# Expert 0's first layer in three column passes, with everything beyond 512 rows behind branches

## The chip, the cores and the metric

The kernel runs on one core of a Trainium2 chip. The metric is the device time of one execution in microseconds (us). The kernel before takes 761.73 us (median of 3 runs, 760.68 to 761.96).

A core has a matrix engine (TensorE, PE in the rows), a vector engine (VectorE, DVE), an engine for activation functions (ScalarE, ACT), GpSimd (POOL), which here also issues gathers and scatters, and SyncE (SP), which issues loads. Each engine works through its own instructions in order; they meet by semaphores.

## The reference

Attention with a causal mask and a bias from cumulated positive scores over 8 batches, 8 heads, 576 positions and head size 64; then a mixture of 8 experts over the 4608 rows of its output:

```python
cum = np.cumsum(np.maximum(s, 0.0), axis=-1)
scores = np.where(causal, -1e9, q @ k.T / sqrt(64) + np.minimum(-(cum[..., :, None] - cum[..., None, :]), 0.0))
x = softmax(scores) @ v                        # then 4608 rows x 512, all heads beside each other
logits = normalize(x) @ normalize(expert_emb).T / tau
expert = argmax(logits, 1); gate = softmax(logits)[expert]
for e in range(8):
    h = np.maximum(x[expert == e] @ w1[e], 0.0)   # 512 -> 1024
    out[expert == e] = gate * (h @ w2[e])         # 1024 -> 512
```

Results are float32.

## The kernel before, in words

The 64 pairs of batch and head are done one after the other in `step(n)`. When a batch is through, its rows are routed: `rank1` to `rank3` give every row a rank within its expert, and five scatters (L662, issued by GpSimd) write the rows to a list xs in HBM, each expert's part in order of rank.

An expert has at most 640 rows in five tiles t of 128. For each, `xload` gathers the rows (L730), `xtr` transposes them on TensorE (four f32 transposes, L756), `xcv` splits them in two float16 halves: xH by a cast on ScalarE (L762) and xL by a subtraction on VectorE (L764). `xstat` takes the sums that the gate needs: a square on ScalarE (L742) and three small operations on VectorE (L739, L740, L77); the gate's logits are nine more (L89 to L97), its weights four (L103 to L106).

Every product is of split float16 halves in three matmuls (xH with wH, xL with wH, xH with wL). The first layer is `l1(m, e, lo, hi)`, m = 0 to 7, 12 matmuls (L859) each over the columns lo to hi, followed by a Relu on ScalarE (L863) for the high half and a subtraction on VectorE (L864) for the low half of h. Its PSUM tile h comes from a pool of two. The second layer is `l2(e, t)`: 24 matmuls of 512 columns (L916), scaling on VectorE (L923) and a scatter to the output (L924).

Rows beyond 512 are a class of their own. `l1a` does the first layer of rows 512 to 575 in 96 matmuls of 64 columns (L882, in `lpart`), always. `l1b` does rows 576 to 639 behind a branch on TensorE and otherwise issues one matmul as a dummy (L900). `lrect` makes the Relu (L888) and the subtraction (L889) of either. `l2t` does tile 4 of the second layer: if there are over 576 rows with 24 full matmuls, if not with a dummy (L939) and 96 matmuls of 64 columns (L945), whose result `l2u` turns back by four transposes (L953) in the next expert. `classes` compares each expert's count with 576, `size` loads the result to TensorE.

Weights come by SyncE's queue (`wissue`), in tiles of 128x512 float32. ScalarE squares them (`wsq`, L814), a small chain gives a scale (`wnorm`, a matmul L825 and five or six operations L826 to L832), `wcv` converts to the high half on ScalarE (L842) and `wlow` takes the low half on VectorE (L850) and issues the load that reuses the space. With `hold`, `wcv` leaves its low halves in a list for a later `wlow`; without, it flushes the whole list.

Expert 0 starts before all rows are routed. When six batches are ranked, its next free rank is raised to at least SPL = 384, so that its first 384 rows don't change any more, and they are gathered as tiles 0 to 2. `l1(0..2)` over these columns stand in the tails of the last attention steps (64 to 66), `l1(3..7)` behind them, `l2(0, 0)` and `l2(0, 1)` follow, and in a second pass the columns 384 to 511, with `l1a(0)` behind m = 1 and `l2(0, 2)` behind m = 3. The order in every engine's queue is the order in which the code is written.

From the reference's inputs, expert 0 has 337 rows in the first six batches, 404 in seven, 468 in eight.

## Time and profile before

| | us |
|---|---|
| median of 3 runs (lowest, highest) | 761.73 (760.68, 761.96) |
| the profiled execution | 760.44 |
| its span, from the first to the last instruction | 758.3 |
| TensorE busy in it | 743.6 (98%) |
| VectorE, ScalarE, GpSimd busy | 527.9 (70%), 568.6 (75%), 393.8 (52%) |

The profile is of one execution. An engine's busy time is the union of its instructions; a row of the timeline gives the start, the length, the engine, the line and the tiles of an instruction or of several alike that follow one another, and in brackets how long the engine was idle before and whose end released it. Matmuls overlap: one that takes 0.38 us lets the next begin after 0.22, so prices are taken from start to start. Attention ends near 345 us; the change lies between about 320 and 403 us.

### The profile page before, as it was taken

The numbers are of one execution on the slowest core, as the hardware profiler recorded it, in microseconds if no ns is written. First come the engines' busy times: TensorE is split into PE (matmuls) and PEld (weight loads), VectorE is DVE, ScalarE is ACT, GpSimd is POOL, SyncE is SP. The second block draws the span as 40 slices with busy tenths as digits, with TensorE's granted clock in tenths as the row PEclk, the third lists the DMA queues.
The fourth block names the chain that finished last, engine by engine and source line by source line (L and its number), as shares of the span: only waits on it lengthen the run. The fifth ranks groups of instructions, "written<-read, shape, count | busy, mean of one in ns | idle before, by whom it ended". The sixth has DMA issues, their size and how long they took to land. (4 is left out here: it accounts for less than half of the span.)

```text
span 758.3 us, 21143 instructions
## 1 busy us (share of the span) xinstructions
PE 743.6 (98%) x8097; PEld 536.9 (71%) x8097; DVE 527.9 (70%) x1799; ACT 568.6 (75%) x1027; POOL 393.8 (52%) x375
## 2 busy tenths in 40 slices
...
GB/s 148 180 190 189 174 180 207 172 212 169 213 184 207 164 225 163 183 233 168 204 117 128 192 161 195 183 141 140 181 176 129 188 171 198 162 126 103 12 15 57
DMA packets 75993, 124.00 MB, mean 164 GB/s; under 512 B 38818, under 2 KB 39222, under 8 KB 75024
## 3 DMA queue, kind: packets, MB, share of 16 engines
...
## 5 line engine op out<-in xcount | busy, mean ns | idle before, releaser
L245 POOL TENSOR_TENSOR PL<-P 128x576 f16<-128x576 f32 (+2 forms) x128 | 204.5, 1718 | 12.5 <-ACT P L491 8.1
L859 PE MATMUL h<-xH,wt 128*128 128x512 f16 (+2 forms) x576 | 159.3, 355 | 0.7 <-DVE hq L864 0.2
L924 POOL DMA_INDIRECT out<-Kx,xj x39 | 43.7, 1122 | 201.3 <-DVE Kx L923 168.8
L859 PEld LDWEIGHTS <-wt 128*128 128x128 f16 x864 | 79.4, 98 | 83.8 <-issue 2.3
L519 PE MATMUL om<-vh,P 128*128 128x73 f16 x960 | 106.8, 199 | 0.9 <-DVE xt L544 0.6
L520 PE MATMUL om<-vl,P 128*128 128x72 f16 x960 | 106.2, 196 | 0.0
L521 PE MATMUL om<-vh,PL 128*128 128x73 f16 x960 | 106.0, 197 | 0.0
L355 PE MATMUL s<-qkb 96*128 96x288 f32 (+4 forms) x272 | 96.3, 368 | 1.5 <-DVE M L363 0.9
L730 POOL DMA_INDIRECT Qx<-xs,idx x40 | 44.3, 1106 | 99.4 <-ACT vjunk L814 56.1
L520 PEld LDWEIGHTS <-P 128*128 128x128 bf16 x960 | 94.7, 99 | 1.6 <-issue 1.1
L519 PEld LDWEIGHTS <-P 128*128 128x128 bf16 x960 | 93.7, 99 | 0.7 <-DVE xt L544 0.4
L521 PEld LDWEIGHTS <-PL 128*128 128x128 f16 x960 | 93.8, 98 | 0.0
L859 PE MATMUL h<-xL,wt 128*128 128x512 f16 (+1 forms) x256 | 90.5, 359 | 0.0
L916 PE MATMUL pxs<-wt,hq 128*128 128x512 f16 x360 | 88.8, 379 | 0.3 <-DVE wt L850 0.3
L916 PE MATMUL pxs<-wt,hp 128*128 128x512 f16 x288 | 77.8, 379 | 0.0
L363 DVE CUSTOM_DVE_ANT_0 junk<-s,mS 128x448 bf16<-128x448 f32 (+3 forms) x144 | 74.0, 521 | 5.1 <-PE s L355 2.8
L923 DVE TENSOR_SCALAR Kx<-pxs,xj,idx 128x512 f32<-128x512 f32 x39 | 31.5, 808 | 54.2 <-PE pxs L916 31.2
L494 ACT ACTIVATE P<-tb 128x1024 f32<-128x1024 f32 x64 | 65.2, 1018 | 4.6 <-PE tb L460 2.8
L916 PEld LDWEIGHTS <-hq 128*128 128x128 f16 x360 | 35.2, 98 | 41.8
L457 PE MATMUL tb<-QC,KC 128*128 128x448 f32 (+3 forms) x256 | 63.4, 307 | 0.0
L453 PE MATMUL tb<-qkb 128*128 128x448 f32 (+3 forms) x256 | 61.2, 287 | 0.0
L842 ACT ACTIVATE wt<-ring,idx 128x512 f16<-128x512 f32 x80 | 53.3, 710 | 8.9 <-DVE idx L829 8.9
...
## 6 DMA issues: line engine op xcount, KB each, us to landing
...
```

The costliest lines, as they stand in the source:

```text
L245: nc.gpsimd.tensor_tensor(out, a, b_, op=ALU.subtract)
L355: nc.tensor.matmul(out, G[g]["QB"][0:96, h, 128 * i:128 * i + 128], G[g]["KB"][0:96, h, lo:hi], start=True, stop=True)
L363: nc.vector.tensor_tensor_reduce(out=jk, in0=src, in1=ms, scale=1.0, scalar=NEG, op0=ALU.add, op1=ALU.max, accum_out=MP[n // 2][:, n % 2, ...
L453: nc.tensor.matmul(out, G[g]["KB"][:, h, ks:ks + 128], G[g]["QB"][:, h, 64 + qlo:64 + qhi], start=start, stop=False)
L457: nc.tensor.matmul(out, HD[n]["KC"][:, ks:ks + 128], HD[n]["QC"][:, qlo:qhi], start=False, stop=stop)
L494: nc.scalar.activation(HD[n]["P32"][:, 576:1600], HD[n]["tb"], AF.Exp, scale=0.125)
L519: nc.tensor.matmul(out, lh, vh[:, kb], start=(kb == 0), stop=False)
L520: nc.tensor.matmul(out[:, u:u + 72], lh, vl[:, kb], start=False, stop=False)
L521: nc.tensor.matmul(out, ll, vh[:, kb], start=False, stop=(kb == j))
L842: nc.scalar.activation(h, a, AF.Copy, scale=s)
L859: nc.tensor.matmul(h, w[:, 128 * c:128 * c + 128], x[:, c, lo:hi], start=(c == 0 and k == 0), stop=(c == 3 and k == 2))
L916: nc.tensor.matmul(y, h, w, start=(m == 0 and k == 0), stop=(m == 7 and k == 2))
```

## The change

The constant SPL becomes 256 and SPM = 384 is new. Expert 0's first pass covers columns 0 to 255 (tiles 0 and 1, gathered after six batches, rank raised to at least 256). After seven batches its rank is raised to at least 384, tile 2 is gathered in step 64, transposed and split in m = 6 of the first pass, and a second pass of eight m does columns 256 to 383. The third pass does columns 384 to 511 in the loop over m for e = 0, without `l1a` and `l2` in it; `l2(0, 2)` now stands ahead of it, right behind `l2(0, 1)`. All rows of expert 0 beyond 512 are behind branches: `l1t` for the first layer, with two dummies and two `lrect`, and `l2z` for the second. For this, `classes` adds 64 to expert 0's count. Squares, conversions, statistics, rank and gate operations are spread anew over the m. In `setup`, the rows 255 and 383 of xs are zeroed, where it was row 383 alone.

```diff
@@ -43,7 +43,9 @@
 CAP = 640
 MAIN = 512
 HALF = 64
-SPL = 384
+SPL = 256
+SPM = 384
+NF = SPM // 128
 NBIG = 1 << 20
 XSH = 4
 
@@ -632,9 +634,9 @@
             nc.vector.tensor_tensor(R["T"], R["pr"][:, 0:40].rearrange("p (j e) -> p j e", j=5),
                                     base.unsqueeze(1).to_broadcast([128, 5, NE]), op=ALU.add)
             nc.vector.tensor_add(base, base, R["pr"][:, 40:40 + NE])
-            if b == nb - 3:
+            if nb - 4 < b < nb - 1:
                 nc.vector.tensor_copy(IX["cnt0"][:, 0:1], base[:, 0:1])
-                nc.vector.tensor_scalar(base[:, 0:1], base[:, 0:1], float(SPL), None, op0=ALU.max)
+                nc.vector.tensor_scalar(base[:, 0:1], base[:, 0:1], float(SPL if b == nb - 3 else SPM), None, op0=ALU.max)
 
         def rank2():
             nc.vector.tensor_tensor(R["T"], R["T"], R["oh"], op=ALU.mult)
...
@@ -866,6 +873,7 @@
     def classes():
         t = IX["b1"]
         nc.vector.tensor_sub(t, base, ebase)
+        nc.vector.tensor_scalar(t[:, 0:1], t[:, 0:1], float(HALF), None, op0=ALU.add)
         nc.vector.tensor_single_scalar(shared["cn"], t, float(MAIN + HALF), op=ALU.is_gt)
 
     def size(e):
@@ -899,6 +907,25 @@
         with arm.Else():
             nc.tensor.matmul(h, wt(1, 0)[0][:, 0:128], X[("H", e)][:, 0, 0:MAIN], start=True, stop=True)
         lrect(1, h)
+
+    def l1t():
+        h = ps_t.tile([128, 2, 512], F32, tag="t", name="h")
+        with tc.If(X["n", 0] == 1) as arm:
+            for u in range(2):
+                lpart(0, u, h[:, u])
+        with arm.Else():
+            for u in range(2):
+                nc.tensor.matmul(h[:, u], wt(1, 0)[0][:, 0:128], X[("H", 0)][:, 0, 0:MAIN], start=True, stop=True)
+        for u in range(2):
+            lrect(u, h[:, u])
+
+    def l2z():
+        y = pxs()
+        with tc.If(X["n", 0] == 1) as arm:
+            l2m(NTL - 1, y)
+        with arm.Else():
+            nc.tensor.matmul(y, hrows(0, 0)[0], wt(2, 0)[0], start=True, stop=True)
+        X["y", 0] = y
 
     def l2h(e, t):
         shared["on"] = ps_m.tile([128, 512], F32, tag="m", name="on")
...
@@ -1171,7 +1198,7 @@
             wlow(1 if n == NH - 1 else 99)
         k = n - NH + 8
         if k > 7:
-            wsq((12, 14, 14)[k - 8])
+            wsq((13, 15, 16)[k - 8])
         if live:
             emm(n)
         sb(n, m)
@@ -1218,11 +1245,10 @@
             xcv(0, 0)
             for f in (norm1, norm2, norm3):
                 f(n - 2)
-            for t in range(1, 3):
-                xtr(0, t, pxs())
-                xcv(0, t)
+            xtr(0, 1, pxs())
+            xcv(0, 1)
         if k > 0:
-            wsq((0, 2, 3, 6, 8, 8, 9, 10, 12, 14, 16)[k])
+            wsq((0, 2, 3, 6, 8, 8, 9, 11, 14, 16, 16)[k])
             wcv((0, 0, 0, 0, 0, 1, 2, 2, 1, 2, 0)[k], True)
         brk[0] = False
         if n < NH:
@@ -1242,6 +1268,8 @@
         for _ in range(SCN[c8] if n < NH - 22 else n - NH + 3 if NH - 3 < n < NH else 1 + (c8 > 5) + 4 * (n > NH - 6)):
             scatter()
         later()
+        if n == NH:
+            xload(0, 2)
         if live and c == 0:
             addl(g + 1, True)
         if live and c == 1:
@@ -1265,11 +1293,13 @@
             HT["Kx"] = const.tile([128, 4, DM], F32, tag="KC0", name="Kx")
             HT["Qx"] = const.tile([128, 3 * XR + DM], F32, tag="QC0", name="Qx")
             wissue(11)
-            xinfo(0, 0, SPL // 128)
+            xinfo(0, 0, NF)
         if k == 5:
             wnorm(HD[n]["ta"])
-            for t in range(3):
+            for t in range(2):
                 xload(0, t)
+        if k in (6, 7):
+            wissue((13, 15)[k - 6])
         if k == 7:
             xtr(0, 0, pxs())
         if 8 <= k < 11:
@@ -1305,24 +1335,30 @@
     for n in range(3, NH + 3):
         step(n)
     for m in range(3, 8):
-        l1(m, 0, 0, SPL, partial(some, 12) if m == 3 else wnorm if m == 4 else None)
-        if 2 < m < 6:
+        l1(m, 0, 0, SPL, partial(some, 12) if m == 5 else wnorm if m == 4 else None)
+        if m < 6:
             wlow(1)
-        if m > 3:
-            wcv((2, 1, 2, 3)[m - 4], m == 4)
-        if 3 < m < 7:
-            xstat(0, m - 4)
-        if m == 4:
+        wcv((0, 2, 2, 1, 1)[m - 3], m < 6)
+        if m == 6:
+            xtr(0, 2, pxs())
+            xcv(0, 2)
             some(4)
-            xinfo(0, SPL // 128, NTL)
-            xload(0, 3)
-        if m == 5:
-            xload(0, 4)
+            xinfo(0, NF, NTL)
+        if m == 7:
             classes()
+    assert not (mq or tasks or first or late or scats)
+    for m in range(8):
+        l1(m, 0, SPL, SPM)
+        if m in (0, 2):
+            wcv(1)
+        if m in (1, 4, 6):
+            t = (1, 4, 6).index(m)
+            xstat(0, t)
+            if t < 2:
+                xload(0, 3 + t)
         if m == 7:
             for f in X[("g", 0, 0)][0:2]:
                 f()
-    assert not (mq or tasks or first or late or scats)
     xinfo(1, 0, NTL)
     xload(1, 2)
 
@@ -1343,20 +1379,23 @@
     l2(0, 0, {3: opening})
     wsq(21)
     l2(0, 1, {2: third, 7: fourth})
-    l1b(0, pxm())
+    wsq(24)
+    l2(0, 2)
+    l1t()
     for e in range(NE):
         nx = e + 1 < NE
         w2, w1 = 16 * e + 8, 16 * e + 16
         for m in range(8):
-            l1(m, e, 0 if e else SPL, MAIN)
-            if e and m == 1:
+            l1(m, e, 0 if e else SPM, MAIN)
+            if e > 1 and m == 1:
                 l2u(e - 1)
-            if m == (2 if e else 1):
+            if e == 1 and m == 0:
+                l2o(0, NTL - 1, X["y", 0])
+            if e and m == 2:
                 l1a(e)
-                if e:
-                    size(e)
+                size(e)
             if e == 1:
-                wsq(w2 + (6, 8)[m] if m < 2 else w1 + (0, 0, 0, 0, 1, 4)[m - 2])
+                wsq(w2 + (4, 6, 8)[m] if m < 3 else w1 + (0, 0, 0, 1, 4)[m - 3])
                 wcv((2, 0, 0, 2, 2, 2, 2, 0)[m])
                 if m == 2:
                     wnorm()
@@ -1381,10 +1420,7 @@
                 xprep(1, m // 3 - 1, pxm())
                 xload(1, 2 + m // 3)
             if e == 0 and m in (1, 3, 4, 5):
-                X[("g", 0, SPL // 128)][(1, 3, 4, 5).index(m)]()
-            if e == 0 and m == 3:
-                wsq(24)
-                l2(0, 2)
+                X[("g", 0, NF)][(1, 3, 4, 5).index(m)]()
             if e > 0 and m < 4:
                 X[("g", e, 0)][m]()
             if not nx and m == 5:
...
@@ -1414,7 +1450,8 @@
                     if t == 3:
                         wnorm()
                     wcv(3)
-                    wsq(24 + 2 * (t - 2))
+                    if t == 4:
+                        wsq(26)
                 else:
                     if t == 1 + (e == 1):
                         wnorm()
@@ -1426,6 +1463,8 @@
                         wnorm()
             if t + 1 < NTL:
                 l2(e, t)
+            elif not e:
+                l2z()
             elif nx:
                 l2t(e)
             else:
```


What this moves in the queues, at three places. First ScalarE, from the Relu of `l1(0)` (hv) on; the squares read `ring` and write `vjunk`, conversions write `wt`. Before:

```order
L863 ACTIVATE hv<-h 128x384
L842 ACTIVATE wt<-rv,idx 128x512
L814 ACTIVATE vjunk,idx<-ring 128x512 x2
L863 ACTIVATE hp<-h 128x384
L842 ACTIVATE wt<-rv,idx 128x512
L842 ACTIVATE wt<-mS,idx 128x512
L863 ACTIVATE hq<-h 128x384
L814 ACTIVATE vjunk,idx<-ring 128x512 x2
```

and of the changed kernel:

```order
L870 ACTIVATE hv<-h 128x256
L819 ACTIVATE vjunk,idx<-ring 128x512
L847 ACTIVATE wt<-rv,idx 128x512
L819 ACTIVATE vjunk,idx<-ring 128x512
L870 ACTIVATE hp<-h 128x256
L819 ACTIVATE vjunk,idx<-ring 128x512
L821 CAST idx<-idx 128x8
L847 ACTIVATE wt<-rv,idx 128x512
L847 ACTIVATE wt<-mS,idx 128x512
L870 ACTIVATE hq<-h 128x256
L870 ACTIVATE hp<-h 128x256
```

Between the first and the second Relu there are two squares and a conversion in either, one of the squares now ahead of the conversion; between the second and the third there is now a square and a small cast more, and two conversions as before.

Second VectorE, from the subtraction of m = 5 (hq) to that of m = 7 of the first pass (hv) and the one behind it. Before:

```order
L864 SCALAR_TENSOR_TENSOR hq<-h,hq 128x384
L850 SCALAR_TENSOR_TENSOR wt<-mS,idx,wt 128x512
L850 SCALAR_TENSOR_TENSOR wt<-ring,idx,wt 128x512 x3
L739 SCALAR_TENSOR_TENSOR xj<-Qx,idx 128x1
L740 COPY xj<-Qx 128x2
L77 TENSOR_REDUCE xj<-Qx 128x8
L868 TENSOR_TENSOR idx<-base,ebase 128x8
L869 TENSOR_SCALAR cn<-idx 128x8
L864 SCALAR_TENSOR_TENSOR hp<-h,hp 128x384
L850 SCALAR_TENSOR_TENSOR wt<-ring,idx,wt 128x512 x2
L739 SCALAR_TENSOR_TENSOR xj<-Qx,idx 128x1
L740 COPY xj<-Qx 128x2
```

and of the changed kernel:

```order
L871 SCALAR_TENSOR_TENSOR hq<-h,hq 128x256
L855 SCALAR_TENSOR_TENSOR wt<-mS,idx,wt 128x512
L871 SCALAR_TENSOR_TENSOR hp<-h,hp 128x256
L855 SCALAR_TENSOR_TENSOR wt<-ring,idx,wt 128x512 x5
L769 TENSOR_TENSOR xL<-pxs,xH 128x4x128
L871 SCALAR_TENSOR_TENSOR hv<-h,hv 128x256
L855 SCALAR_TENSOR_TENSOR wt<-ring,idx,wt 128x512
L875 TENSOR_TENSOR idx<-base,ebase 128x8
L876 TENSOR_SCALAR idx<-idx 128x1
L877 TENSOR_SCALAR cn<-idx 128x8
L871 SCALAR_TENSOR_TENSOR hv<-h,hv 128x128
```

The low halves of five W2 tiles (`wt<-ring`) now stand together between the subtractions of m = 6 and m = 7, and xL of tile 2 behind them, which in the kernel before was done with tiles 0 and 1 in step 63. The xstats of this place have moved to the second pass.

Third VectorE in the pass over columns 384 to 511, around the gate's logits of the last two tiles. Before:

```order
L764 TENSOR_TENSOR xL<-pxm,xH 128x4x128
L89 RECIPROCAL idx<-idx 128x2
L90 TENSOR_TENSOR idx<-idx,xj 128x2
L91 TENSOR_TENSOR idx<-idx 128x2
L92 SCALAR_TENSOR_TENSOR idx<-idx,xj 128x2
L93 RECIPROCAL idx<-idx 128x2
L94 TENSOR_SCALAR idx<-idx,itau 128x2
L95 TENSOR_TENSOR xj<-xj,idx 128x16
L96 TENSOR_REDUCE idx<-xj 128x2
L97 TENSOR_TENSOR xj<-xj,idx 128x16
L923 TENSOR_SCALAR Kx<-pxs,xj,idx 128x512
L864 SCALAR_TENSOR_TENSOR hq<-h,hq 128x128 x2
```

and of the changed kernel:

```order
L769 TENSOR_TENSOR xL<-pxm,xH 128x4x128
L91 RECIPROCAL idx<-idx 128x2
L92 TENSOR_TENSOR idx<-idx,xj 128x2
L93 TENSOR_TENSOR idx<-idx 128x2
L94 SCALAR_TENSOR_TENSOR idx<-idx,xj 128x2
L95 RECIPROCAL idx<-idx 128x2
L96 TENSOR_SCALAR idx<-idx,itau 128x2
L97 TENSOR_TENSOR xj<-xj,idx 128x16
L98 TENSOR_REDUCE idx<-xj 128x2
L99 TENSOR_TENSOR xj<-xj,idx 128x16
L871 SCALAR_TENSOR_TENSOR hq<-h,hq 128x128 x2
L105 TENSOR_REDUCE idx<-idx 128x2
```

The scaling of `l2(0, 2)` (Kx) that stood between the logits and the subtractions of m = 4 and 5 (hq) is gone from here; it now stands ahead of the pass.

## Rows read from the trace of the kernel before

**Rows 1.** The page: the span, and the engines' busy time, its share of the span and the number of instructions.

```profile
span 758.3 us, 21143 instructions
PE 743.6 (98%) x8097; PEld 536.9 (71%) x8097; DVE 527.9 (70%) x1799; ACT 568.6 (75%) x1027; POOL 393.8 (52%) x375
```

**Rows 2.** The list of waits of TensorE from 400 to 720 us: what was waited for, us in total, times, longest.

```profile
PE h L859 <- DVE hq L864: 0.2, 1, 0.2
```

**Rows 3.** The timeline of TensorE around the change: start, length, engine, line, operation, tiles written and read, shape, count.

```profile
339.83 0.21 PE L519 MATMUL om<-vh,P 128*128 128x73 f16 x1 [0.21 <-DVE xt L544]
...
341.34 0.33 PE L859 MATMUL h<-xH,wt 128*128 128x384 f16 x1
...
343.29 0.20 PE L519 MATMUL om<-vh,P 128*128 128x73 f16 x1
...
358.86 0.81 PE L916 MATMUL pxs<-wt,hv 128*128 128x512 f16 x3
...
370.67 0.38 PE L900 MATMUL pxm<-xH,wt 128*128 128x512 f16 x1
370.89 0.22 PE L859 MATMUL h<-xH,wt 128*128 128x128 f16 x1
...
372.67 0.22 PE L859 MATMUL h<-xH,wt 128*128 128x128 f16 x1
...
373.34 0.19 PE L882 MATMUL pxs<-xH,wt 128*128 128x64 f16 x1
...
376.14 0.22 PE L859 MATMUL h<-xH,wt 128*128 128x128 f16 x1
...
377.93 0.81 PE L916 MATMUL pxs<-wt,hv 128*128 128x512 f16 x3
...
383.11 0.22 PE L859 MATMUL h<-xH,wt 128*128 128x128 f16 x1
...
386.88 0.81 PE L916 MATMUL pxs<-wt,hv 128*128 128x512 f16 x3
...
394.84 0.35 PE L945 MATMUL pxm<-hq,wt 128*128 128x64 f16 x6 [1.97 <-DVE xL L764]
...
397.65 0.38 PE L859 MATMUL h<-xH,wt 128*128 128x512 f16 x1
...
402.83 0.60 PE L953 MATMUL pxs<-ident,hq 128*64 128x128 f32 x4
403.27 0.38 PE L859 MATMUL h<-xH,wt 128*128 128x512 f16 x1
```

**Rows 4.** Windows: from and to, length, busy time of PE, PEld (weight loads), DVE, ACT and POOL with their counts, granted clock, DMA share and GB/s.

```profile
320.00:330.00 10.00, 9.94 (x186) 9.81 (x186) 7.49 (x23) 8.86 (x20) 7.83 (x7) 1.00 0.60 188
345.00:350.00 5.00, 5.00 (x41) 3.11 (x40) 3.93 (x13) 4.72 (x11) 0.70 (x3) 1.00 0.78 274
355.00:360.00 5.00, 5.00 (x31) 2.64 (x29) 4.45 (x15) 5.00 (x13) 2.35 (x3) 1.00 0.66 224
360.00:365.00 5.00, 4.66 (x23) 1.98 (x22) 4.87 (x14) 3.29 (x9) 3.20 (x3) 1.00 0.87 284
390.00:395.00 5.00, 3.04 (x22) 1.52 (x20) 4.02 (x9) 4.94 (x12) 1.01 (x1) 1.00 0.52 159
395.00:400.00 5.00, 5.00 (x107) 3.73 (x105) 2.22 (x4) 2.24 (x6) 0.00 (x0) 1.00 0.66 211
```

**Rows 5.** The timeline of ScalarE in the first pass and behind `l1a`, columns as in rows 3.

```profile
345.25 0.49 ACT L863 ACTIVATE hv<-h 128x384 f16<-128x384 f32 x1 [1.79 <-DVE wt L850]
345.63 0.71 ACT L842 ACTIVATE wt<-rv,idx 128x512 f16<-128x512 f32 x1
346.25 0.62 ACT L814 ACTIVATE vjunk<-ring 128x512 bf16<-128x512 f32 x1
...
346.99 0.63 ACT L814 ACTIVATE vjunk<-ring 128x512 bf16<-128x512 f32 x1
...
376.34 0.60 ACT L888 ACTIVATE hq<-pxs 128x512 f16<-128x512 f32 x1 [2.52 <-PE pxs L882]
```

**Rows 6.** The timeline of VectorE in the first and the second pass.

```profile
350.19 0.20 DVE L632 TENSOR_TENSOR om<-om,base 128x40 f32<-128x40 f32 x1
...
351.29 0.18 DVE L657 TENSOR_SCALAR idx<-idx 128x40 int32<-128x40 f32 x1
...
357.08 2.07 DVE L850 SCALAR_TENSOR_TENSOR wt<-ring,idx,wt 128x512 f16<-128x512 f32 x3
...
376.97 0.69 DVE L889 SCALAR_TENSOR_TENSOR hq<-pxs,hq 128x512 f16<-128x512 f32 x1 [2.21 <-ACT hq L888]
...
379.69 0.15 DVE L89 RECIPROCAL idx<-idx 128x2 f32<-128x2 f32 x1
...
381.35 0.18 DVE L97 TENSOR_TENSOR xj<-xj,idx 128x16 f32<-128x16 f32 x1
```

**Rows 7.** The list of waits of TensorE from 340 to 400 us, columns as in rows 2.

```profile
PE pxs L756 <- DVE xL L764: 0.5, 1, 0.5
PE pxs L916 <- DVE wt L850: 0.3, 1, 0.3
```

**Rows 8.** DMA issues from 318 to 402 us: tiles, queue, kind, count, and the median us from issue to landing.

```profile
Qx<-xs,idx POOLq DMA_INDIRECT x10, 6.6
xs<-xt,pos POOLq DMA_INDIRECT x10, 4.4
```

27 lines of the change are left out of this document (16 added, 11 removed).

## The prediction

> **What bounds the kernel now.** I read the page first: TensorE is busy for 743.6 of 758.3 us [rows 1], and in every window read its granted clock is 1.00, the 2.4 GHz level [rows 4]. So time can only be won by giving TensorE less work or by removing one of its few waits, and is lost by a new wait. Then the list of waits behind 400 us: one wait of 0.2 us until 720 us [rows 2]. From expert 1's first matmul on, everything is therefore shifted by whatever happens before it, unchanged in length; the question is when that matmul starts, 397.65 in the trace of before [rows 3]. Third, the windows of 5 us around the change: TensorE is full, but VectorE is busy for 4.45 and 4.87 of 5 us and ScalarE for 4.72 and 5.00 in stretches of the first pass and just behind it [rows 4]. The three engines are balanced there; whatever shortens TensorE's share without shortening the others' makes it wait for them. Last, the timelines of TensorE, ScalarE and VectorE for the prices [rows 3, 5, 6].
>
> **How the layer-1 loop waits.** A tile h lives in a pool of two, so l1(m) can't start before the Relu (ScalarE) and the subtraction behind it (VectorE) have read l1(m-2)'s h. What stands between two Relus in ScalarE's queue sets the pace as soon as it takes longer than the matmuls.
>
> **Prices.** Twelve matmuls of 384 columns take 1.95 us (341.34 to 343.29), twelve of 128 columns 0.67 (372.67 to 373.34) [rows 3]. For 256 columns, which the trace lacks, the bounds are these two; I take the middle, 1.31. So 8 x (1.31 + 0.67) = 15.8 us replace 8 x 1.95 = 15.6 of before's first pass; the 128 columns of rows 384 to 511 remain. 96 matmuls of 64 columns take 2.80 (373.34 to 376.14), 24 of 512 columns 5.18 (377.93 to 383.11), a dummy 0.22 (370.67 to 370.89), four f32 transposes 0.44 (402.83 to 403.27) [rows 3]. A square on ScalarE takes 0.74 from start to start, a weight conversion 0.62, a Relu of 384 columns 0.38 before the next one starts, from which I estimate 0.3 for 256 [rows 5]. A low-half subtraction of a weight tile takes 0.66 on VectorE (three end to end in 2.07), a 128x512 subtraction 0.69, the eight operations of the ranks 1.3 (350.19 to 351.47), the nine of the gate's logits 1.84 (379.69 to 381.53) [rows 6].
>
> The trace of before also says which branch arms are taken: l2t's short arm ran for expert 0 (the 64-column matmuls L945 [rows 3]). From the reference's inputs expert 0 has 337, 404 and 468 rows after six, seven and eight batches. Before, the raise to 384 made 515 ranks of it, so rows beyond 512 were in use; after, 404 is over 384, no rank is wasted, and 468 are left. All three branches go the dummy way.
>
> **Stage 1, both first passes, until l2(0,0).** TensorE work: before 17.52 (341.34 to 358.86). After: 17.52 + 15.8 - 15.6 + 0.44 for one tile's transposes that now stand in here, 18.1. These transposes (0.44) and the 0.21 of waiting at 339.83 are gone ahead of it; both together, 0.7, is my estimate for the earlier start, with 0 as the other end, if what is waited for doesn't move [rows 3].
> - Pass 1 waits. ScalarE's first Relu starts when the low halves that it overwrites are done: 345.25 before [rows 5], 344.5 after. Behind it stand square, conversion, square (2.1 us) and then square, a small cast, two conversions (2.1), with a Relu of 0.3 ahead of each; each period is 2.4 us against 1.31 of matmuls. l1(2), l1(3) and l1(4) wait about 0.6, 1.1 and 1.15. Later the ranks' 1.3 us, moved from m=3 to m=5, and a weight tile's low half stand ahead of one subtraction: 0.45. Sum 3.3.
> - Between the passes. xL of the third row tile, which pass 2's second matmul reads, stands on VectorE behind five low halves of W2 (5 x 0.66 = 3.3) that begin only after the Relu subtraction of m=6. That subtraction ends about 0.9 before TensorE ends pass 1; 3.3 + 0.69 - 0.9 = 3.1 us of waiting. Queued behind the waiting matmul is all of pass 2.
> - Pass 2 has 0.67 of matmuls per m, while VectorE does a subtraction, and a low half (0.66) in m = 0 to 2 and the three xstats; three waits of about 0.35, sum 1.0.
>
> Stage 1 ends at 341.34 - 0.7 + 18.1 + 7.4 = 366.1, 7.3 later than 358.86.
>
> **Stage 2, l2(0,0) and l2(0,1).** Before 12.03 (358.86 to 370.89), of it 0.34 waiting for a low half [rows 7], which are all done by then, and 0.22 of the dummy, both gone. Now l2(0,2) follows at once and needs a PSUM bank of two, held by the fifth row tile's transposes until ScalarE (cast behind a square) and VectorE have split it; before, the wait of 0.47 at that place [rows 7] had a dummy and twelve matmuls ahead of it (1.3 us). Without this cover 1.5. Together -0.56 + 1.5 = +0.9.
>
> **Stage 3, third pass.** Before 15.99 (370.89 to 386.88): l1a 2.80, l2(0,2) 5.18, a wait of 0.47, and 7.54 of the rest. After: l2(0,2) 5.18, two dummies 0.43, the rest 7.54, and two new waits. First, lrect now runs twice in a row on the dummies' output, Relu 0.60 and subtraction 0.69 each [rows 5, 6], with the bank shared by both halves, ahead of hv's subtraction for which l1(2) waits: 2 x 0.65 + 0.6, less the 0.67 for l1(1) that covers, with hv's own 0.4: 1.85. Before, the first of them lay beside l1a's 2.80. Second, the gate's nine operations (1.84) and xL (0.69) stand ahead of hq's subtraction: before all of it lay beside l2(0,2)'s 5.18; now beside 0.67 of l1 and transposes: 2.5. Sum: 5.18 + 0.43 + 7.54 + 4.35 = 17.5, +1.5.
>
> **Stage 4, until expert 1.** Before 10.77 (386.88 to 397.65). The 96 matmuls of 64 columns (394.84 to 397.65, 2.81) and the wait of 1.97 ahead of them go: -4.78 [rows 3]. Their bank z, which waited for expert 1's fifth xL, is no longer used, and nothing else waits for it before expert 1's first layer ends. In expert 1 the four transposes of l2u go: -0.44.
>
> **Sum.** +7.3 + 0.9 + 1.5 - 4.8 - 0.4 = +4.5 on the profiled execution's 760.44 (span 758.3 and 2.1 around it): 764.9. The median of the runs is 1.29 higher; on that basis 766.2. Seen the other way, TensorE's own work falls by about 5.7 us (2.80 + 2.81 + 0.44, less 0.2 for columns and 0.2 for one dummy more) and old waits of 3 us go, but 13.3 us of new waits come: 7.4 + 1.5 + 4.35.
>
> **Costed at nothing.** Five small operations more on VectorE for the seventh batch's ranks, 0.16 each, stand in the attention, where VectorE is busy for 7.49 of 10 us and TensorE is full [rows 4]; without that cover 0.8. Two weight loads issued earlier on SyncE's queue, and the squares and conversions that move with them on ScalarE, are inside the periods above; a load late would add its own lateness to stage 1. One branch fewer on TensorE: nothing, the dummy at 370.67 follows the transposes without a gap [rows 3].
>
> **A rule that speaks against the change.** The trace shows 56 ns a matmul of 128 columns (0.67 us for twelve [rows 3]). The Trainium skill, "TensorE: Matmul & The Clock Gate", section "Back-to-back issue gap", says that in a stream where each matmul loads its weights, 128 columns sustain about 81 ns and 512 about 131. By that rule the 96 matmuls of the added narrow pass would cost 2.4 us more than by the row and the time would be about 768.5; but the same rows show 216 ns at 512 columns, so the trace disagrees at both widths, and the sum goes by the rows.
>
> **Rivals.**
> 1. The other engines keep up (chance 0.1). For it: TensorE was full at the same VectorE and ScalarE loads [rows 4], and the low halves could run ahead. Against it: their queues are fixed and busy for 9 tenths already. Time: stage 1 -0.7 + 0.6 = -0.1, then -0.56, -2.84, -4.78, -0.44: -8.7, so 753.0.
> 2. Part of the waits is covered (chance 0.2): the third pass's 4.35 vanish, because VectorE and ScalarE gain a lead beside the 5.18 of l2(0,2), or half of stage 1's 7.4 goes. Against it: what is late in the third pass stands behind subtractions of that pass in the same queue, so a lead gained earlier doesn't help it. Time about 761.8, no change; the point from which the sign turns is 9 of the 13.3 us of new waits.
> 3. Gathers come late (chance 0.1). Rows land 6.6 us after issue in the median [rows 8]. The fourth and fifth tiles and expert 1's second are now issued later beside the weights' loads, the last only when ScalarE is through the third pass's casts; 7 us behind it the transposes of that tile are due. 1.7 at the median, up to 4 with a slow landing: 768 to 770.
> 4. The branches are taken after all (0.02): if expert 0 had over 512 ranks, 192 x 29 ns + 24 x 216 ns = 10.8 us would come back, less the dummies: 776.
> 5. The clock falls in a new gap (0.03). The rows show full clock right through the 1.97 us gap and behind it [rows 3, 4]; the new one is 3.1 with 1.0 us gaps around it. At 1.2 instead of 2.4 GHz pass 2's 5.4 us would double: 771. The Trainium skill, "TensorE: Matmul & The Clock Gate", section "HAM oscillation — how this bites in real kernels", says that idle stretches between bursts lower the clock; by that rule this rival would hold, and the trace so far shows no case of it.
>
> **Numbers.** Forecast 766.2, chance 0.55, own range 763.3 to 768.5 (a fifth of the new waits either way; the unknown 256-column price would be up to 5 us either way between its bounds, but 29, 56, 163 and 216 ns a matmul at 64, 128, 384 and 512 columns lie on a line, which leaves some 0.3). Fewer than 2 in 10 are outside 757 to 770. A difference of 0.2%, about 1.5 us, is what a measurement of this kernel tells from none: faster (below 760.2) takes rival 1 and a third of rival 2, 0.17; within it (to 763.3) half of rival 2 and the forecast's own lower edge, 0.12; slower the rest, 0.71.
>
> **What would show it.** Right: idle time of TensorE released by Relu subtractions before the third l1 of pass 1; one wait near 3 us at the start of pass 2, released by xL; about 1.5 ahead of l2(0,2); two of 2 us in the third pass; expert 1's first matmul near 402; no 64-column matmuls for expert 0. Wrong: pass 2 starts without a wait, or expert 1 starts before 398, or 64-column matmuls of expert 0 appear.

## The result and the profile after

The changed kernel takes 772.12 us (median of 4 runs, 770.43 to 773.59) against 761.26 for the kernel before (median of 4 runs on the same chip, 760.68 to 761.96). The ratio is 1.0141, its 95% interval 1.0117 to 1.0166: slower by 1.4%. The forecast had the sign, but 766.2 is 5.9 us too little, and 772.12 lies outside both of its ranges (763.3 to 768.5, and 757 to 770). The profiled execution took 771.44 us, its span is 769.7.

The first two lines of the page, the answer to [rows 1]:

```profile
span 769.7 us, 20959 instructions
PE 740.6 (96%) x7998; PEld 537.6 (70%) x7998; DVE 530.9 (69%) x1812; ACT 570.2 (74%) x1035; POOL 394.2 (51%) x375
```

TensorE has 3.0 us less to do (740.6 after 743.6), the span is 11.4 us longer. So TensorE idles 14.4 us more, and the list of its waits from 345 to 420 us, 14.3 us in sum, names most of that (what was waited for, us in total, times, longest):

```profile
PE h L866 <- DVE xL L769: 2.9, 1, 2.9
PE h L866 <- DVE hq L871: 2.3, 1, 2.3
PE om L830 <- ACT idx L821: 2.3, 1, 2.3
PE h L866 <- DVE hq L897: 1.7, 1, 1.7
PE h L866 <- DVE hp L871: 1.5, 3, 1.1
PE pxs L943 <- DVE xL L769: 1.4, 1, 1.4
PE h L918 <- issue: 0.8, 1, 0.8
PE h L866 <- DVE hv L871: 0.7, 2, 0.5
PE h L866 <- ACT hp L870: 0.4, 1, 0.4
PE h L866 <- DVE wt L855: 0.3, 1, 0.3
```

In the kernel before, the same stretch held waits of 0.5, 0.3, 0.2 and the 1.97 ahead of L945 [rows 2, 3, 7]. The timeline of TensorE shows where each new one stands (columns as in rows 3):

```profile
342.31 0.27 PE L866 MATMUL h<-xH,wt 128*128 128x256 f16 x1
...
349.64 0.27 PE L866 MATMUL h<-xH,wt 128*128 128x256 f16 x1 [1.07 <-DVE hp L871]
...
361.13 0.22 PE L866 MATMUL h<-xL,wt 128*128 128x128 f16 x1 [2.92 <-DVE xL L769]
...
380.57 0.81 PE L943 MATMUL pxs<-wt,hv 128*128 128x512 f16 x3 [1.40 <-DVE xL L769]
...
386.69 0.60 PE L918 MATMUL h<-xH,wt 128*128 128x512 f16 x2 [0.78 <-issue]
390.06 0.23 PE L866 MATMUL h<-xH,wt 128*128 128x128 f16 x1 [1.66 <-DVE hq L897]
396.55 0.22 PE L866 MATMUL h<-xH,wt 128*128 128x128 f16 x1 [2.34 <-DVE hq L871]
...
397.32 1.06 PE L759 MATMUL pxm<-ident,Qx 128*128 128x128 f32 x4
...
406.25 0.38 PE L866 MATMUL h<-xH,wt 128*128 128x512 f16 x1
...
414.02 0.19 PE L890 MATMUL pxs<-xH,wt 128*128 128x64 f16 x1
...
419.26 0.17 PE L830 MATMUL om<-idx,onesb 128*128 128x8 bf16 x1 [2.28 <-ACT idx L821]
```

From top to bottom: the first matmul of pass 1; a wait in pass 1; the start of pass 2 (its second matmul reads xL of tile 2); l2(0,2); l1t's dummies; the third pass with the waits behind lrect and behind the gate's logits; the first matmul of expert 1 (406.25, where before had 397.65); its `l1a`; and a wait in expert 1 that the prediction doesn't have. The four transposes at 397.32 take 1.06 us, in [rows 3] 0.60: TensorE ran on the lower of its two levels, 1.2 GHz (the granted clock is 0.50 from 397.0 to 400.5). The windows of the third pass and of expert 1's begin show it in the granted clock (columns as in rows 4):

```profile
385.00:390.00 5.00, 2.63 (x23) 1.44 (x20) 2.19 (x4) 1.92 (x6) 0.98 (x1) 1.00 0.17 59
390.00:395.00 5.00, 4.13 (x64) 3.88 (x65) 3.42 (x16) 2.99 (x11) 0.41 (x1) 1.00 0.01 2
395.00:400.00 5.00, 3.45 (x31) 3.38 (x31) 3.45 (x18) 2.12 (x8) 1.27 (x2) 0.71 0.25 64
400.00:405.00 5.00, 5.00 (x26) 2.41 (x25) 3.70 (x13) 3.61 (x8) 0.39 (x1) 0.95 0.23 59
```

Put beside the trace of before, stage by stage, the 11.4 us come out as follows (us; before's times are the starts in [rows 3] and the same rows further on in its timeline, after's those above, and for l2(0,0) 367.77):

| stretch | before | after | difference | predicted |
|---|---|---|---|---|
| start of l1(0) | 341.34 | 342.31 | +0.97 | -0.7 |
| stage 1: l1(0) to l2(0,0) | 17.52 | 25.46 | +7.94 | +8.0 |
| stage 2: to the third pass (before) or l2(0,2) (after) | 12.03 | 12.80 | +0.77 | +0.9 |
| stage 3: to l2(0,3) | 15.99 | 19.81 | +3.82 | +1.5 |
| stage 4: to expert 1 | 10.77 | 5.87 | -4.90 | -4.8 |
| expert 1 up to `l1a` (l2u's transposes) | 8.21 | 7.77 | -0.44 | -0.44 |
| expert 1, `l1a` to m = 3 | 2.82 | 5.26 | +2.44 | 0 |
| the rest of expert 1, and the end | | | +0.8 | 0 |

From expert 2 on, every `l1a` starts 11.05 or 11.06 us later than before: but for 0.35 at the end, all of it happens ahead of 465 us. Four terms hold; the start, stage 3 and expert 1 are off by 1.7, 2.3 and 2.4 us, all to the same side.

### The profile page after: what moved, and what is told of

The parts are those of the page before. It is cut to its first block, busy times and chain, and to the rows that moved or that the text cites. A ratio compares the mean times of both kernels' runs of the same rounds, so it can differ in the third digit from the quotient of the medians.

```text
span 769.7 us, 20959 instructions
## 1 busy us (share of the span) xinstructions
PE 740.6 (96%) x7998; PEld 537.6 (70%) x7998; DVE 530.9 (69%) x1812; ACT 570.2 (74%) x1035; POOL 394.2 (51%) x375
## 5 line engine op out<-in xcount | busy, mean ns | idle before, releaser
L866 PE MATMUL h<-xH,wt 128*128 128x512 f16 (+2 forms) x640 | 161.8, 338 | 7.6 <-DVE hq L871 2.6
L866 PEld LDWEIGHTS <-wt 128*128 128x128 f16 x960 | 85.7, 98 | 93.6 <-issue 14.3
L866 PE MATMUL h<-xL,wt 128*128 128x512 f16 (+1 forms) x288 | 96.8, 345 | 2.9 <-DVE xL L769 2.9
L855 DVE SCALAR_TENSOR_TENSOR wt<-ring,idx,wt 128x512 f16<-128x512 f32 x80 | 56.8, 747 | 5.4 <-ACT wt L847 5.2
```

What stands on the lines that cost most here:

```text
L855: nc.vector.scalar_tensor_tensor(l, a, s, h, op0=ALU.mult, op1=ALU.subtract)
L866: nc.tensor.matmul(h, w[:, 128 * c:128 * c + 128], x[:, c, lo:hi], start=(c == 0 and k == 0), stop=(c == 3 and k == 2))
```

## The experiments

Unless said otherwise an experiment is an edit of the changed kernel. Times are medians; a ratio is to the kernel before on the same chip, with its 95% interval. The chips differ a little (the kernel before has medians of 761.26 to 762.06 on them), so a difference of two experiments' medians is good to some 0.8 us. The changed kernel's interval is 1.0117 to 1.0166; those of 2 and of 4 to 8 overlap it, so that there the time alone proves no difference and the reading rests on the trace. Of the changed kernel's variants only 1, 3 and 9 are clear of it.

**1. Expert 1's squares as they were.** This undoes the one part of the change that moved ScalarE's squares behind expert 0.

```diff
             if e == 1:
-                wsq(w2 + (4, 6, 8)[m] if m < 3 else w1 + (0, 0, 0, 1, 4)[m - 3])
+                wsq(w2 + (6, 8)[m] if m < 2 else w1 + (0, 0, 0, 0, 1, 4)[m - 2])
...
-                    if t == 4:
-                        wsq(26)
+                    wsq(24 + 2 * (t - 2))
```

> The changed kernel with one part undone: the squares of expert 1's W2 tiles are issued where they were before (up to 28 by the last tile of expert 0, up to 32 by m = 1 of expert 1, instead of 26 and 32 by m = 2). Theory: TensorE's wait of 2.28 us in expert 1, for the cast that ends the chain of squares, exists because two squares stand later in ScalarE's queue; undone, that wait goes, the distance from expert 1's first layer to expert 2's is that of before again (2.9 us shorter), and the time falls from 772.1 to about 769.3. Rival: ScalarE reaches expert 1 late as a whole, so that the squares come late wherever they stand; then the wait shrinks by less than 1 us and the time stays above 771.

768.45 us, ratio 1.0093 [1.0075, 1.011]: 3.7 us less than the changed kernel. The wait for `idx` L821 is gone from the list, and from `l1a` to m = 3 it is 2.83 us again (5.26 with the change, 2.82 before). ScalarE's timeline of the changed kernel says why:

```profile
415.28 0.58 ACT L870 ACTIVATE hq<-h 128x512 f16<-128x512 f32 x1
417.02 0.60 ACT L896 ACTIVATE hq<-pxs 128x512 f16<-128x512 f32 x1 [1.16 <-PE pxs L890]
417.51 0.62 ACT L819 ACTIVATE vjunk<-ring 128x512 bf16<-128x512 f32 x1
...
418.26 0.63 ACT L819 ACTIVATE vjunk<-rw 128x512 bf16<-128x512 f32 x1
...
419.01 0.20 ACT L821 CAST idx<-idx 128x8 bf16<-128x8 f32 x1
```

The two squares now stand behind the Relu that has to wait for `l1a`, and the cast of the norms, which a matmul on TensorE needs, stands behind the squares. Before, the cast was done at 406.1, ahead of that Relu:

```profile
405.94 0.20 ACT L816 CAST idx<-idx 128x8 bf16<-128x8 f32 x1
```

The theory holds; this was the largest single missed term.

**2. xL ahead of the low halves.** The third tile's transposes and split are put ahead of the five conversions of m = 6.

```diff
-        wcv((0, 2, 2, 1, 1)[m - 3], m < 6)
         if m == 6:
...
             xcv(0, 2)
+        wcv((0, 2, 2, 1, 1)[m - 3], m < 6)
+        if m == 6:
             some(4)
```

> The changed kernel with the transposes and the split of expert 0's tile 2 written ahead of the conversion that flushes five low halves of W2, in m = 6 of the first pass. Theory: the wait of 2.92 us at pass 2's second matmul is those low halves (5 x 0.66 us) ahead of xL on VectorE; with xL first it falls below 0.5, and about 2.5 us of time are saved (about 769.6), the low halves then lying beside pass 2. Rival: VectorE is the bound of both passes together, so that the low halves only move the wait into pass 2's own subtractions: the sum of TensorE's waits from 340 to 368 us stays within 1 us of 6.5, and the time at 771 or above.

771.93 us, 1.0133 [1.0116, 1.015]. The wait for xL is gone and another stands in its place:

```profile
361.49 0.22 PE L866 MATMUL h<-xH,wt 128*128 128x128 f16 x1 [2.65 <-DVE hv L871]
```

The subtraction of m = 7's h is behind the same five low halves. The rival holds: VectorE's queue as a whole is late here, not the one tile that happens to be waited for.

**3. The low halves spread over pass 2.** As 2, and the low halves are held and done one at a time.

```diff
-        wcv((0, 2, 2, 1, 1)[m - 3], m < 6)
...
+        wcv((0, 2, 2, 1, 1)[m - 3], True)
...
         if m in (0, 2):
-            wcv(1)
+            wcv(1, True)
+        wlow(1)
```

> The changed kernel with tile 2's split ahead of the low halves, as in the run with xL first, and these held back and done one per m of the second pass. Theory: with xL first the wait moved to hv's subtraction behind the five low halves (2.65 us); one low half and one subtraction of 128 columns take 0.86 us of VectorE per m against 0.67 of matmuls, so the wait falls to the difference, some 0.2 per m: 1.5 to 2.5 us less in the second pass than in the changed kernel, and 1.4 more where the clock no longer falls: 768.5 to 770.5. Rival: the second layer needs the low halves and waits for them instead: 771 or above.

768.53 us, 1.0085 [1.0056, 1.0113]. The largest wait of pass 2 falls from 2.92 to 0.34, and l1(0) to l2(0,0) takes 23.05 instead of 25.46. So the five low halves in one block are the backlog, and spreading them is what helps. Of the 7.94 us that stage 1 had grown by this returns 2.41.

**4. The gate's logits beside l2(0,2).** They are issued in the middle of l2(0,2), where 5.2 us of matmuls cover them.

```diff
-    l2(0, 2)
+    l2(0, 2, {4: logits})
...
-            if e == 0 and m in (1, 3, 4, 5):
-                X[("g", 0, NF)][(1, 3, 4, 5).index(m)]()
```

> The changed kernel with the thirteen gate operations of expert 0's last two tiles written into l2(0,2), ahead of the third pass, instead of between its m. Theory: the wait of 2.34 us in the third pass (for hq's subtraction behind the nine logits operations) is only their place in VectorE's queue; beside l2(0,2)'s 5.2 us, where VectorE is busy for 1.2 of 5 us, they cost nothing: the wait falls below 0.3, the time by 2 us (770), and by up to 1.4 more where TensorE's clock had fallen behind that gap. Rival: VectorE's work just moves, and another subtraction or xL of the third pass is late instead: less than 1 us.

773.17 us, 1.015 [1.0123, 1.0178]; no gain. In the third pass the wait of 2.34 shrinks and a new one follows:

```profile
394.75 0.22 PE L866 MATMUL h<-xH,wt 128*128 128x128 f16 x1 [0.59 <-DVE hq L871]
...
398.89 0.67 PE L759 MATMUL pxs<-ident,Qx 128*128 128x128 f32 x4 [2.20 <-DMA Qx<-xs,idx]
```

The rows of the next tile of expert 1 are gathered in m = 3 of the same pass, and GpSimd issues this gather at 394.54, in the changed kernel at 394.59: with TensorE sooner at its transposes, the rows are late for them. Rival 3 of the prediction, late gathers, is true here, and was covered by the wait ahead of it in the changed kernel.

**5. l1t ahead of l2(0,2).** Its two lrect then lie beside l2(0,2).

```diff
-    l2(0, 2)
     l1t()
+    l2(0, 2)
```

> The changed kernel with l1t written ahead of l2(0,2) instead of behind it. Theory: the 1.66 us that the third pass waits for the two lrect of the dummies' output then lie beside l2(0,2), and what TensorE needs for its jump lies beside the wait for xL of the fifth tile that is there anyway: 1.7 to 2.5 us less (770). Rival: the dummies now wait for the fifth tile's xL and l2(0,2) behind them for a second PSUM bank: the wait of 1.4 ahead of l2(0,2) grows by what the third pass loses, no change.

769.53 us, 1.0109 [1.0077, 1.0141]: 2.6 us less than the changed kernel. In place of the 1.66 behind lrect stands a wait of 0.65 for hp's subtraction, the one for xL ahead of l2(0,2) falls from 1.40 to 0.97, the "issue" of 0.78 is gone: 2.2 together. As the theory had it.

**6. No branch.** This kernel leaves out the arm of l1t that computes rows of expert 0 beyond 512; the dummies stay.

```diff
-        with tc.If(X["n", 0] == 1) as arm:
-            for u in range(2):
-                lpart(0, u, h[:, u])
-        with arm.Else():
-            for u in range(2):
-                nc.tensor.matmul(h[:, u], ...)
+        for u in range(2):
+            nc.tensor.matmul(h[:, u], ...)
```

> The changed kernel with the branch of l1t taken out: its two dummy matmuls are issued always (the arm for over 512 rows of expert 0, which these inputs never take, is left out). Theory: the 0.78 us that TensorE waits ahead of the dummies, for nothing that the profile names (issue), is the jump over the 384 instructions of the other arm; without it the dummies follow l2(0,2) with no wait, and about 0.8 us are saved (771.3), 2 us more if with the shorter stretch of idling TensorE's clock stays at 2.4 GHz behind 397 us. Rival: the dummies wait for their PSUM tile or for the count on TensorE: the wait stays, under the name of another engine or of issue, and the time with it.

771.13 us, 1.0135 [1.0116, 1.0155]. No "issue" is left among the waits, all others stay. The time falls by 1.0 against the changed kernel, which is within the spread of its runs. The row of 0.78 goes as expected; but in 5, with the branch in place behind l2(0,1), it is gone as well, so the branch is what makes such a wait possible, and its size depends on more than the branch.

**7. The start: rank operations, gather, or subtraction.** Ahead of l1(0) the changed kernel shows one long row on VectorE, beside GpSimd's (the first two rows are VectorE's, the last GpSimd's):

```profile
332.20 0.53 DVE L546 TENSOR_TENSOR xt<-om,z 128x360 f32<-128x360 f32 x1
332.64 3.77 DVE L503 TENSOR_TENSOR PL<-P 128x576 f16<-128x576 f32 x1
```

```profile
332.78 3.01 POOL L247 TENSOR_TENSOR PL<-P 128x576 f16<-128x576 f32 x2
```

In the kernel before the same subtraction took 1.01, and GpSimd's pair began after it:

```profile
331.91 1.01 DVE L501 TENSOR_TENSOR PL<-P 128x576 f16<-128x576 f32 x1
```

```profile
333.85 3.00 POOL L245 TENSOR_TENSOR PL<-P 128x576 f16<-128x576 f32 x2
```

Three edits ask what moved them together. The first puts the three rank operations of the third tile behind the attention:

```diff
-            if nb - 4 < b < nb - 1:
-                t = slice(0, 2) if b == nb - 3 else slice(2, 3)
+            if b == nb - 3:
+                t = slice(0, 2)
```

> The changed kernel with three of the five small rank operations that were added for the seventh batch moved from step 62 to just ahead of the gather of tile 2. Theory: expert 0's first layer starts 0.97 us late (342.31 instead of 341.34) because these operations delay VectorE's subtraction of attention's P (line 503) to 332.64, just when GpSimd begins its own of 3.0 us, and VectorE's then lasts 3.77 instead of 0.75 to 1.0 us; without three of them it starts ahead of GpSimd's, lasts about 1 us, and the first layer starts at 341.3 or before; time about 1 to 1.7 us less. Rival: the operations themselves are the delay (0.5 us) and the long subtraction is chance: then it stays above 3 us and the time changes by 0.5 at most.

771.5 us, 1.0139 [1.0121, 1.0157]; the subtraction starts earlier, lasts 4.20 and ends at the same time. That theory fell. The second gives GpSimd the third gather back, at its old place in step 60:

```diff
                 xload(0, t)
+            nc.gpsimd.indirect_dma_start(out=HT["Qx"][:, 2 * XR:3 * XR].bitcast(I32), ...)
```

> The changed kernel with a third, useless gather in step 61, where the kernel before gathered tile 2 (it fills a buffer that is filled again later). The run with the rank operations moved showed that these don't set the length of VectorE's subtraction of P: it began 0.46 us earlier and ended at the same 336.3, 0.55 behind the end of GpSimd's own subtraction. New theory: the missing gather lets GpSimd come to its subtraction 1.1 us earlier (332.78 instead of 333.85), ahead of VectorE's, which then waits for its end; with the gather back it starts near 334, VectorE's takes 0.75 to 1.0 us, and expert 0's first layer starts at 341.4 or before instead of 342.3; the time falls by 0.5 to 1.7 us. Rival: the long subtraction depends on something else, as the data or the weight load on VectorE's queue: it stays above 3 us.

774.67 us, 1.0176 [1.0145, 1.0208]. The subtraction is short again:

```profile
332.80 0.75 DVE L503 TENSOR_TENSOR PL<-P 128x576 f16<-128x576 f32 x1
```

So the length comes from GpSimd's subtraction beside it. GpSimd's rows show where its 1.1 us come from: before, a gather (329.22, 1.01 us) stands ahead of the pair that starts at 330.24; with the change that pair starts at 329.01. But this run does not restore the old times, as its expectation had it: GpSimd's pair starts at 337.18 instead of near 334, behind a scatter that waited 3.14 us for xt. GpSimd is late from there on: a matmul in the attention waits 1.5 us for its PL and one of its subtractions runs beside a low half in pass 1 that takes 3.55. The third edit leaves the queues and takes only the collision away; step 62's VectorE share of the subtraction goes to GpSimd:

```diff
-        return 1024 if NH - 7 < n < NH - 1 else 1600
+        return 1024 if NH - 7 < n < NH - 2 else 1600
```

> The changed kernel with VectorE's subtraction of P in step 62 (the one that lasts 3.77 us beside GpSimd's) given to GpSimd, which does the whole of it in that step. Theory: VectorE's long subtraction is only its waiting for GpSimd to be through; without it VectorE goes on at once, TensorE's waits of 0.73 (for vl) and 0.58 us (for xt) ahead of l1(0) go, and the stretch from 326 us to l1(0) is 1 to 1.3 us shorter. Rival: GpSimd, now longer by about 1 us, makes TensorE wait for PL instead: the stretch is as long as in the changed kernel or longer. Time 771 in the one case, 772 to 773 in the other.

770.61 us, 1.0117 [1.0102, 1.0132]: 1.5 less than the changed kernel, of which the trace gives 0.83 to the start (1 to 1.3 was expected). Measured from one matmul of the attention (tb<-qkb of 448 columns, at 303.4 to 303.6 in all of them), l1(0) starts after 37.94 us in the kernel before, 38.84 with the change, 38.86 with late ranks, 38.00 with the gather, 38.01 with this edit. The collision costs 0.83; without it the start is where it was.

**8. The clock.** Dummies fill the two large gaps: 25 of 256 columns ahead of pass 2, 10 of 512 in the third pass.

```diff
+    warm(25, SPL)
     for m in range(8):
         l1(m, 0, SPL, SPM)
...
+            if e == 0 and m == 5:
+                warm(10, MAIN)
```

> The changed kernel with matmuls that compute nothing used in its two longest waits: 25 of 256 columns (2.7 us) ahead of the second pass, where TensorE waits 2.92 us for xL, and 10 of 512 columns (2.2 us) in the third pass behind m = 5, where it waits 2.34 us. Theory: the falls of the granted clock behind these waits, which the windows show at 361 to 367 us or at 396 to 401 us, follow from TensorE standing idle, and each costs 1 to 1.5 us; with TensorE kept busy the windows from 340 to 420 us all show 1.00 and the time falls by 1 to 2.5 us although the kernel does more. Rival: the clock falls for another reason, or the dummies delay what follows as much as a slow clock does: the time stays within 1 us of 772.1 or is longer.

770.34 us, 1.0116 [1.0083, 1.015]: 1.8 us less, with more work for TensorE. The windows that were at 0.71 and 0.95:

```profile
395.00:400.00 5.00, 4.79 (x45) 3.25 (x44) 4.03 (x20) 3.01 (x10) 1.03 (x1) 1.00 0.22 61
400.00:405.00 5.00, 5.00 (x27) 2.56 (x26) 4.11 (x13) 3.48 (x7) 0.26 (x1) 1.00 0.48 163
```

From the first matmul behind the gate's wait to expert 1 it is 8.32 us (395.78 to 404.10), with the change 9.70 (396.55 to 406.25). The wait ahead of pass 2 ends 18.82 us behind l1(0) in either kernel; only what TensorE did in it differs. One profile without a fall is little, because the fall behind the gate's wait doesn't come every time. But the other profiles say the same: of the changed kernel and its variants with a wait of 2.34 there, the five whose clock fell took 9.60 to 9.71 us from its end to expert 1, the four whose clock did not fall 8.09 to 8.70. And over all runs, the mean granted clock is 0.996 to 0.998 here and 0.990 to 0.997 in the changed kernel. So idle time lowers the clock, if not each time, and the lower level costs some 0.9 to 1.6 us behind the gate's wait.

**9. All of it together.** First version: 1, 3, 4, 5, the gather of 7, two branches with a shorter jump instead of one, and the fifth tile prepared earlier.

> All together on the changed kernel: expert 1's squares back, the gate operations in l2(0,2), l1t ahead of l2(0,2) with two branches of 192 instructions each, the useless third gather, tile 2's split ahead of the low halves and these one per m of the second pass, and the fifth tile prepared at m = 4 instead of 7 of l2(0,1). If each lost piece has its own cause, the savings add up: 2.9 + 2.3 + 1.7 + 0.9 + 1.4 for the fifth tile, 1 for the spread and 1.4 for a clock that doesn't fall, 11.6 of 772.1: about 760.5, level with the kernel before. If ScalarE and VectorE are the bound of the whole stretch, the waits come back elsewhere and it stays above 764.

766.18 us (6 runs), 1.0059 [1.0037, 1.008]: the rival's case. Pass 2 has no wait over 0.34, but the gather's costs from 7 and one of 4's are back, and two short jumps wait no less than one long one:

```profile
PE pxs L759 <- DMA Qx<-xs,idx: 2.2, 2, 2.0
...
PE om L523 <- POOL PL L247: 1.5, 1, 1.5
PE h L917 <- issue: 1.3, 1, 1.3
```

Second version: without the gather, with the single branch, and expert 1's first tile prepared beside l2(0,2), so that its next gather is issued early:

```diff
     l1t()
+    l2(0, 2, {2: first0, 5: logits})
...
-            if e == 0 and m in (3, 6):
-                xprep(1, m // 3 - 1, pxm())
-                xload(1, 2 + m // 3)
+            if e == 0 and m == 3:
+                xprep(1, 1, pxm())
+                xload(1, 4)
```

> The changed kernel with: expert 1's squares back, the gate operations and expert 1's first row tile in l2(0,2) (so that its gather of the fourth tile starts 4 us earlier), l1t with its single branch ahead of l2(0,2), tile 2's split ahead of the low halves and these one per m of the second pass, the fifth tile at m = 4 of l2(0,1); no third gather. In the run of all together the second pass had no wait above 0.3 us left, 2.0 us were lost for a gather in the third pass, 1.3 at the two branches and 2.3 for GpSimd at the start. If these are the last ones, the time is 766.2 - 2.0 - 0.5 - 2.3 + 0.8 = 762.2, at the kernel before or a little under it. If the stretch is bound by VectorE and ScalarE, the gather's and GpSimd's time comes back as other waits: 764 or above.

763.43 us (10 runs), 1.0014 [0.9999, 1.0029]: level with the kernel before, 8.7 us under the changed one. What is left of its waits from 345 to 420 us:

```profile
PE h L918 <- issue: 1.6, 1, 1.6
PE h L866 <- DVE hp L871: 1.3, 2, 1.1
PE h L866 <- DVE hv L871: 1.3, 4, 0.5
PE h L866 <- DVE hq L871: 1.3, 3, 0.6
...
PE h L866 <- ACT hp L870: 0.4, 1, 0.4
```

These are above all the jump and pass 1 (0.48, 1.06 and 0.44, as in the changed kernel). By these rows the narrower first pass costs about what the saved work brings; no run tests that by itself. Ahead of this stretch the collision of 7 is still there (VectorE's subtraction takes 3.77): that edit is not part of this version.

**10. l2(0,2) first, in the kernel before.** The one reordering, without the passes (an edit of the kernel before).

```diff
     l1b(0, pxm())
+    wsq(24)
+    l2(0, 2)
     for e in range(NE):
...
-            if e == 0 and m == 3:
-                wsq(24)
-                l2(0, 2)
```

> The kernel before with one part of the change alone: l2(0,2) ahead of the pass over columns 384 to 511 instead of behind its m = 3. Theory: these 24 matmuls are the cover of the gate's logits on VectorE and of expert 1's gathers; without them TensorE waits about 2 us in the pass, for hq's subtraction or for the fourth tile's rows, and the time rises by 1.5 to 3 us (763.3 to 764.8). Rival: the two waits of the third pass come from the two lrect and the dummies that the change brings; then the kernel before loses nothing by this (within 0.7 us of 761.8).

764.85 us (10 runs), 1.0042 [1.0024, 1.006]: 2.8 us over the 762.03 of the kernel before on the same chip. The two waits that the prediction hung on this move appear without the rest of the change, the clock's fall behind the second one too (0.80 and 0.86 from 385 to 395 us):

```profile
PE h L859 <- DVE hq L864: 2.3, 1, 2.3
PE pxm L945 <- DVE xL L764: 1.6, 1, 1.6
PE pxs L916 <- DVE xL L764: 1.1, 1, 1.1
```

**11. The one old wait, in the kernel before.** The 1.97 us ahead of L945 [rows 3] belonged to the bank that expert 1's last tile used. Here the banks of the last two tiles are exchanged.

```diff
-                    xprep(1, t, (pxs if t == 3 else pxm)())
+                    xprep(1, t, (pxm if t == 3 else pxs)())
```

> The kernel before with nothing but the two PSUM banks of expert 1's last two row tiles exchanged: the fourth is transposed into the bank of pool m, the fifth into one of pool s. Theory: the wait of 1.97 us ahead of the 64-column matmuls L945 is for the bank that the fifth tile's transposes hold until its xL is done; exchanged, that bank is free, and only the dummy L939 can still wait, for a bank of pool s: 1 to 2 us less than the kernel before, 760.0 to 761.0, faster than both kernels. Rival: the dummy then waits as long for its own bank, or ScalarE and VectorE are late for expert 1 instead: no change.

761.16 us (11 runs), 0.9989 [0.9978, 0.9999]. The wait is gone; two others, 1.07 and 0.47, hold most of it:

```profile
388.00 0.66 PE L756 MATMUL pxm<-ident,Qx 128*128 128x128 f32 x4 [1.07 <-DVE xL L764]
...
394.77 0.38 PE L939 MATMUL pxs<-wt,hv 128*128 128x512 f16 x1 [0.47 <-DVE Kx L923]
```

From l2(0,0) to expert 1 it is 38.56 us, before 38.79. It is the fastest version measured, by a tenth of a per cent, less than the 0.2% that the prediction took as the bound for telling two kernels apart. Its fastest run (760.47) is no faster than the fastest of the kernel before on the same chip (760.33); what it lacks are the longer ones: 11 of the 23 runs of the kernel before had a mean granted clock of 0.996 and took 762.06 to 764.33, while all 11 runs here had 0.998 or more and took at most 761.67. So the gap of 1.97 us, behind which the profiled execution kept its clock, may lower it in others; no profile of such a run shows where it fell. With expert 0's fifth tile moved to m = 4 of l2(0,1) as well:

> The same with expert 0's fifth row tile also prepared at m = 4 instead of m = 7 of l2(0,1), which in the changed kernel's variants took the wait for its xL away. Theory: the wait of 0.47 us ahead of expert 1's transposes in the second pass goes as well: 0.3 to 0.5 us less than with the banks alone. Rival: its rows land too late for m = 4 (in the kernel before the gather is issued 10 us earlier than the transposes): TensorE then waits for the DMA.

761.75 us (12 runs), 0.9999 [0.9988, 1.0011]: no difference. The tile's rows have not landed there; its transposes wait 1.31 us for the gather.

## Why the prediction was right and wrong

**Right: what bounds the kernel.** TensorE was the engine that counted, and less work for it bought nothing where VectorE and ScalarE could not follow. Rival 1 (the others keep up) is out.

**Right: stage 1, 7.94 of 8.0.** The single waits: 0.48, 1.07 and 0.44 in pass 1 for l1(2) to l1(4) (0.6, 1.1 and 1.15 predicted), 2.92 for xL at pass 2 (3.1 predicted). Twelve matmuls of 256 columns take 1.31 (342.31 to 343.62), as taken from the middle of the bounds. The list counts idle time alone; a matmul of 128 or 256 columns lasts some 0.16 us longer than the step to the next one, and this too is lost at each wait. So the eight waits of over 0.2 us in stage 1, 5.84 in the list, are by this estimate 7.1 us of the stage, where 7.4 was predicted; that l1(4) lost only about half of its 1.15 is hidden in the total. The reason given for pass 2 was half right: xL stood behind five low halves, but 2 shows that m = 7's subtraction did too, so that moving xL alone is worth 0.2 us and spreading the low halves (3) 3.6.

**Right: stages 2 and 4 and l2u.** 1.40 ahead of l2(0,2) (1.5 predicted), the 64-column matmuls and their wait gone. 10 shows that this wait and the one behind the gate's logits belong to the moved l2(0,2), not to the narrower pass.

**Half right: stage 3, +3.8 instead of +1.5.** Both waits named are there at their size, 1.66 (1.85) and 2.34 (2.5). Two steps failed. "One branch fewer on TensorE: nothing" was read from a dummy that followed without a gap [rows 3]; l1t's dummies lie behind a jump over more code (two parts of 96 matmuls instead of one), and TensorE waited 0.78 for nothing that the profile shows. 6 removes the jump and the wait with it; where the jump is kept, the traces show from nothing (5) to 1.63. The Trainium skill, "Runtime: NRT & Kernel Launch", section "Instruction fetch mechanics", says that a taken branch to a page of code that isn't loaded stalls until it is fetched; these rows fit it, though none shows the fetch itself.

The second step is rival 5: that the clock falls in a new gap had a chance of 0.03. It was argued from a gap of 1.97 that left the clock at 1.00 [rows 3, 4], in one execution (see 11), and put at one place. In the profiled runs the clock fell around the start of pass 2 in eight of the nine kernels with a wait of 2.65 to 2.92 there (the changed kernel's own profile is the ninth), in none of the three where 0.26 was left, and not in 8, where dummies filled it. In stage 1 this makes 26.21 to 26.70 us of 25.46 in seven of the eight (the run with the gather has other waits there), so 0.8 to 1.2; behind the gate's wait it is the 1.4 of 8. It happened beside the forecast, not as another outcome: every profiled kernel with these gaps left as they are pays for one or more. The rule weighed there, of "HAM oscillation — how this bites in real kernels" in the Trainium skill's "TensorE: Matmul & The Clock Gate", was the better guide: the traces agree with it that idle stretches lower the clock, here single waits of 2.2 to 2.9 us, though not each of them.

**Wrong: the start, +0.97 instead of -0.7.** The gain of 0.7 was an estimate with 0 as its other end, and 0 is what happened: with 7's third edit l1(0) starts 0.07 later than before. What is waited for did not move: the time of the transposes came back as a wait for VectorE's xt, 0.73 in that run where before it was 0.21 [rows 3].

```profile
339.87 0.21 PE L521 MATMUL om<-vh,P 128*128 128x73 f16 x1 [0.73 <-DVE xt L546]
```

The 0.83 on top were not in the sum at all. The step that failed is the cover of "Costed at nothing": the windows show VectorE with room [rows 4], but not that the gather taken out of GpSimd's queue lets GpSimd's subtraction start earlier, beside VectorE's own. What moves in one queue was counted; what it makes another engine collide with was not. The trace of before shows such meetings (the row of 335.23 below); their price was there to read.

**Wrong: expert 1, +2.44 and more.** That "the squares and conversions that move with them on ScalarE, are inside the periods above" was true of expert 0's pass and not of expert 1's: the diff does two squares of each of its first steps one m later, and "From expert 1's first matmul on, everything is therefore shifted by whatever happens before it, unchanged in length" assumed that nothing there was changed. 1 gives back 2.4 us of it in the trace and 3.7 in the medians.

**The sum.** The misses are 1.7, 2.3, 2.4 and 0.8 us at the end, together with the small ones 6.9 of span: 4.5 predicted, 11.4 found. The range had a fifth of the named new waits as its uncertainty; it had no room for losses that were put at nothing, and these (0.8 for the collision, 0.8 for the jump, 1.4 for the clock and 2.3 for expert 1's squares, 5.3 together) are most of the 6.9.

**Open.** Why the clock falls at the gate's wait of 2.34 in some kernels (six of ten profiled) and not in others, and behind expert 1's wait of 2.28 in three of ten, was not settled; nor are the 0.45 us behind m = 3 of expert 1 and 0.35 at the end traced to a row.
